# Chunk bounds as eight concurrent fp32 products over 576 queries, and a written-out order, in a chunk-selecting attention kernel with a phase mixer

## The chip, the cores and the metric

The kernel runs on one core of one Trainium2 chip. The metric is device time in microseconds from launch to end of one execution; a profile adds the span from the first to the last instruction, which is a little shorter. One core has five engines with a queue each: TensorE (PE; its weight loads are PEld), VectorE (DVE), ScalarE (ACT), GpSimd (POOL) and SyncE (SP, which issues the DMAs here).

## The reference: what is computed

For 4 batches and 8 heads, 768 positions and a head size of 64, each query chooses 6 of 24 chunks of 32 keys by an upper bound on its scores, and attends to the keys of the chosen chunks that are not after it:

```
k_min, k_max = min and max of k over each chunk of 32 keys
ub  = sum over d of max(q * k_min, q * k_max)          # [.., 768, 24]
ub  = where(chunk of query >= chunk, ub, -1e9)
sel = the 6 chunks with the largest ub
attn = softmax(where(sel and causal, q @ k.T / 8, -1e9)) @ v
```

The heads are then laid side by side to x of 4 x 768 x 512, and a mixer follows:

```
theta = x @ w_theta
y = w_tok_r @ (x * cos(theta)) + w_tok_i @ (x * sin(theta))
u = x + y
out = u + max(u @ w_ch, 0)
```

Everything comes in and goes out as fp32. The bounds decide which chunks are chosen, so they are computed in fp32; scores and mixer run in fp16 with fp32 accumulation.

## The kernel before

The work is cut into tasks: `Plan.add` records for each one its engine (or a choice of ACT and DVE), an estimated duration, a key, what it reads and writes, and the buffers it takes. `Plan.order` then plays the tasks through a list scheduler: at each step it takes, among the engines, the task that can start first, and among equals the one with the smaller key. The table `SHIFT` moves the keys of named groups of tasks and biases the choice between ACT and DVE. `Plan.emit` writes the instructions in the order found, and on the chip each engine takes its own instructions in that order.

PSUM has three rings of buffers: "sc" (two, for scores), "av" (one, for attention times values) and "mi" (three banks, for everything else). The stages are:

- `load_kc`, `load_q`, `load_v`: DMAs for a group of four heads (batch b, half g) or a pair of heads.
- `keys`: VectorE takes maximum and minimum over each chunk in a tree (L411, L416, L420); TensorE transposes them (psk, L435); they become `bnd`, with dimension on the partitions, two heads of a pair on the two partition halves (L440). GpSimd casts the keys, and TensorE transposes them (pkt) into `kext`.
- `queries`: TensorE transposes q of a head pair in fp32 (psq, L485). ACT or DVE splits it into two parts by sign with a Relu (`ubq`, L493 and L495), so that the bound becomes two matrix products: one part with the maxima, one with the minima.
- `choice`: for a group of four heads, TensorE multiplies `bnd` by `ubq` (psub, L517), ACT or DVE copies the result to `ubm` (L525), TensorE transposes it back (psut, L532), and VectorE adds the causal mask (L537), finds the eight largest (L547) and compares with the sixth (L558). The result goes beside the cast queries and is turned by a DMA transpose into `qext`, where it acts as a mask inside the score product.
- `attend`: for each of 32 heads, scores (psc, L622), exp on ACT (pt, L631), a triangle mask on GpSimd (L642), the product with the values (psav, L653), a division on VectorE into x (L664, L669).
- `phases`: x transposed (psT, L688), theta (pst, L708), cos and sin on ACT, multiplied by x on VectorE (zz, L722).
- `mixer`: the token products (psy or, in the last batch, psz: L749, L751), u = x + y on VectorE (L761), u transposed (psut, L772, or a DMA), the channel product (pso, L784), the last addition (ot, L789), and the store.
- `token`: a token weight is loaded, cast on GpSimd (a, L809) and transposed (pw, L816).

The mixer of batch b runs between the heads of batch b + 1; the mixer of the last batch stands alone at the end. There are eight groups (b, g) for `choice`. A query in the first 192 positions sees at most six chunks, so it chooses all it may see. The kernel before leaves out the first 128 queries for that reason and covers the other five blocks of 128 in two parts of 256 and 384 columns:

```python
PARTS = ((1, 2), (3, 4, 5))
...
for y in range(2):
    for z, u in enumerate(us):
        nc.tensor.matmul(t[64 * z:64 * z + 64, :],
                         bnd[g][:, y, 2 * z:2 * z + 2, :].rearrange("p x c -> p (x c)"),
                         st[u][:, y, c0:c0 + w], start=(y == 0), stop=(y == 1))
```

Each such matmul contracts over all 128 partitions, which hold both heads of a pair. The sign constant `signs` makes one half of the partitions carry a maximum where the other carries a minimum, and the other way round in the second y.

Of the kernel before, what the change touches and what calls it, by code (L numbers as in the profile page):

```python
# [9 lines left out]
FP32 = mybir.dt.float32  # L10
# [6 lines left out]
class Task:  # L17
    __slots__ = ("i", "eng", "dur", "fn", "key", "deps", "succ", "alloc", "uses", "opts", "lock", "psum",
                 "after_start", "left", "ready", "start", "end", "kind", "group", "bias")


class Plan:
# [9 lines left out]

    LAT = {"PE": 0.22, "ACT": 0.08, "DVE": 0.08, "POOL": 0.08, "SP": 2.0}

    def __init__(self, bufs, in_order, hot, boost, shift):
        self.tasks = []
        self.bufs = bufs
        self.in_order = in_order
        self.count = {}
        self.hot, self.boost = hot, boost  # L40
        self.shift, self.group = shift, None
        self.turn = {}
        self.writers, self.readers = {}, {}
        self.tag_of, self.users = {}, {}

    def add(self, eng, dur, key, fn, r=(), w=(), new=(), after=(), kind=None, lock=False):
        t = Task()
        t.i, t.eng, t.dur, t.fn, t.key, t.kind = len(self.tasks), eng, dur, fn, key, kind
        t.opts = eng if isinstance(eng, dict) else {eng: dur}
        t.lock = lock or eng == "POOL"  # L50
        t.key += self.shift.get(self.group, 0.0)
        t.group = self.group
        t.bias = self.shift.get(("dve", self.group), 0.0)
        t.deps, t.after_start, t.succ, t.alloc, t.uses = set(), set(), [], [], []
        for name, tag in new:
            self.tag_of[name] = tag
            self.turn[name] = self.count.get(tag, 0)
            self.count[tag] = self.turn[name] + 1
            self.users[name] = []
            t.alloc.append(name)  # L60
        names = [n for n, _ in new]
        t.psum = [n[0] for n in r if isinstance(n, tuple) and self.tag_of.get(n[0]) in self.hot]
        if isinstance(eng, dict) or eng in ("ACT", "DVE"):
            if t.psum:
                t.key -= self.boost
        else:
            t.psum = []
        for n in list(r) + list(w) + names:
            base = n[0] if isinstance(n, tuple) and n and n[0] in self.users else n
            if base in self.users and t not in self.users[base]:  # L70
                self.users[base].append(t)
                t.after_start.add(self.users[base][0].i)
                t.uses.append(base)
        for n in r:
            t.deps |= set(self.writers.get(n, ()))
            self.readers.setdefault(n, []).append(t.i)
        for n in list(w):
            t.deps |= set(self.readers.get(n, ()))
            t.deps |= set(self.writers.get(n, ()))
            self.writers[n] = [t.i]  # L80
            self.readers[n] = []
        for n in names:
            self.writers[n] = [t.i]
        t.deps |= set(a.i for a in after)
        t.deps.discard(t.i)
        t.after_start -= t.deps | {t.i}
        self.tasks.append(t)
        return t

    def order(self):  # L90
        T = self.tasks
        for t in T:
            t.left = len(t.deps) + len(t.after_start)
            t.ready = 0.0
            t.start = None
            for d in t.deps:
                T[d].succ.append(t.i)
            for d in t.after_start:
                T[d].succ.append(t.i)
        placed = {}  # L100
        pending = {}
        freed, last = {}, {}
        for n, us in self.users.items():
            pending[n] = len(us)
        free_at = dict.fromkeys(("PE", "ACT", "DVE", "POOL", "SP"), 0.0)
        mode = [None]
        cand = {e: [] for e in free_at}
        for t in T:
            if t.left == 0:
                for e in t.opts:  # L110
                    cand[e].append(t)
        reader, port = {}, 0.0
        n_done, seq = 0, []
        now = 0.0

        def begin(t, e):
            s = max(free_at[e], now, t.ready, port if t.lock else 0.0)
            for n in t.psum:
                if n in reader and reader[n][0] != e:
                    s = max(s, reader[n][1] + 0.1)  # L120
            return s

        while n_done < len(T):
            best = None
            for e, c in cand.items():
                at = max(free_at[e], now)
                pick = None
                for t in c:
                    s = begin(t, e)
                    ok = True  # L130
                    if len(t.opts) > 1:
                        mine = s + t.opts[e] + (t.bias if e == "DVE" else 0.0)
                        for o, d in t.opts.items():
                            if o != e and begin(t, o) + d + (t.bias if o == "DVE" else 0.0) < mine:
                                ok = False
                    own = {}
                    for n in t.alloc:
                        tag = self.tag_of[n]
                        ring = placed.setdefault(tag, [])
                        m = len(ring) + own.get(tag, 0)  # L140
                        own[tag] = own.get(tag, 0) + 1
                        if tag in self.in_order and self.turn[n] != m:
                            ok = False
                            break
                        k = m - self.bufs[tag]
                        if k >= 0:
                            f = freed.get(ring[k])
                            if f is None:
                                ok = False
                                break  # L150
                            s = max(s, f)
                    if not ok:
                        continue
                    if pick is None or (max(s, at + 1e-9), t.key, t.i) < pick[0]:
                        pick = ((max(s, at + 1e-9), t.key, t.i), s, t)
                if pick and (best is None or pick[1] < best[1]):
                    best = pick + (e,)
            assert best is not None, "no task can start"
            _, s, t, _ = best
            for e in t.opts:  # L160
                cand[e].remove(t)
            t.eng = best[3]
            d = t.opts[t.eng]
            if t.kind is not None:
                if mode[0] not in (None, t.kind):
                    d += 1.3
                mode[0] = t.kind
            t.start, t.end = s, s + d
            now = s
            free_at[t.eng] = t.end  # L170
            if t.lock:
                port = t.end
            for n in t.psum:
                reader[n] = (t.eng, max(t.end, reader.get(n, (0, 0.0))[1]))
            lat = self.LAT[t.eng]
            for n in t.alloc:
                placed[self.tag_of[n]].append(n)
            for n in t.uses:
                pending[n] -= 1
                last[n] = max(last.get(n, 0.0), t.end + lat)  # L180
                if pending[n] == 0:
                    freed[n] = last[n]
            for i in t.succ:
                u = T[i]
                u.left -= 1
                same = t.eng != "SP" and list(u.opts) == [t.eng]
                u.ready = max(u.ready, t.start if t.i in u.after_start else t.end + (0.0 if same else lat))
                if u.left == 0:
                    for e in u.opts:
                        cand[e].append(u)  # L190
            seq.append(t)
            n_done += 1
        return seq

    def emit(self):
        for t in self.order():
            t.fn(t.eng) if len(t.opts) > 1 else t.fn()
# [3 lines left out]
def kernel(  # L201
# [19 lines left out]
    NM = 5  # L221
    scale = float(1.0 / np.sqrt(D))
# [17 lines left out]
    qt = P + np.arange(NM)[None, :, None] * P + np.arange(P)[:, None, None]  # L240
    cm_np = np.where(qt // CH >= np.arange(NCH)[None, None, :], 0.0, -1e9).astype(np.float32)
    cm_h = nc.inline_tensor(cm_np.reshape(P, NM * NCH), name="cmask32")
# [5 lines left out]
    cmask32 = const.tile([P, NM, NCH], FP32, name="cmask32", tag="c_cm")  # L248
# [103 lines left out]
    def act_t(n):  # L352
        return 0.19 + n / 1200.0
# [602 lines left out]
```

The softmax here doesn't subtract the row's maximum and nothing guards it: scores larger than these inputs give would overflow.

## Time and profile before

| what | value |
|---|---|
| time, median of 3 runs | 272.23 us (272.11 to 273.69) |
| span of the profiled execution | 270.0 us |
| mean granted TensorE clock | 0.968 |
| psub matmuls L517 | 128 records, 20.8 us busy |
| psut transposes L532 | 40 records, 273 ns median |
| scores L622 | 256 records, 51.7 us busy |
| token products L749 and L751 | 240 records, 45.5 and 45.4 us busy |
| first and last start of psub | 15.8 and 190.3 us |

The page gives for each engine its busy time, its share of the span and its instructions, and then the span in 40 equal slices. Busy time is an average over stages with different limits, so the span has to be cut where the work changes before anything is read from it. Matmuls overlap in the pipeline: the sum of their durations is more than the busy time.

### The profile page before, as it was taken

Reading aid. Unit: us, or ns where it says so; the run is one execution under the profiler, and the core shown is the slowest. Engines: PE = TensorE matmul, PEld = TensorE weight load, DVE = VectorE, ACT = ScalarE, POOL = GpSimd, SP = SyncE. Lnnn points to the kernel's source line nnn. Section 1 sums busy time; section 2 is a strip of 40 time slices with the busy share of each in tenths; the row PEclk is TensorE's granted clock in tenths of the full one; section 3 lists DMA queues with packets and bytes.
Section 4 is the critical chain, followed back from the end, with each engine's and each line's share of the span. In section 5 each row is a group of like instructions: output and inputs, shape, how many; then the busy total and the mean of one; then the engine's idle time right before and its main releaser. Section 6 shows DMA issues by size and latency. Waiting matters only on the chain.

```text
span 270.0 us, 5519 instructions
## 1 busy us (share of the span) xinstructions
PE 240.8 (89%) x2055; PEld 147.8 (55%) x2055; DVE 195.5 (72%) x474; ACT 162.0 (60%) x225; POOL 135.0 (50%) x188
## 2 busy tenths in 40 slices
PE   4896586978689989989999999999999999899993
PEld 1553355666434676655763477666654667434441
DVE  3959689899799594799999985997853436344453
ACT  2349647489559499271938879635687777374000
POOL 7534657668368886968642278536302555100000
PEclk9999598999869999999999999999999999999999
DMA  7897857799989789898988642337180014310123
GB/s 198 199 240 156 213 123 113 199 259 243 252 220 258 191 232 210 185 242 211 257 204 203 121 98 62 70 89 177 22 197 0 19 41 94 141 58 0 41 78 117
DMA packets 90434, 40.71 MB, mean 151 GB/s; under 512 B 83736, under 2 KB 83864, under 8 KB 89736
## 3 DMA queue, kind: packets, MB, share of 16 engines
q1 hardware_dynamic: 90408, 40.37, 61.5%
q8 instruction: 16, 0.26, 0.4%
q14 instruction: 10, 0.08, 0.1%
HBM read 26.20 MB, written 6.29 MB: 120 GB/s over the span
## 4 chain that ended last, share of the span: by engine, by line
PE 56%; DMA 16%; DVE 13%; POOL 8%; issue 3%; SPq 2%; ACT 1%; POOLq 0%; DVEq 0%; ACTq 0%
PE psy L749 8%; PE psy L751 8%; PE psc L622 8%; PE pso L784 6%; PE psub L517 5%; PE psav L653 5%; DMA w<-in_moe_w_tok_r_dram 4%; POOL pt L642 4%; DMA out_dram<-ot 4%; PE pst L708 4%; DMA q<-in_q_dram 3%; DMA w<-in_moe_w_tok_i_dram 3%; PE psq L485 2%; POOL a L809 2%; DVE h L411 2%
## 5 line engine op out<-in xcount | busy, mean ns | idle before, releaser
L631 ACT ACTIVATE pt<-psc 128x1024 f16<-128x1024 f32 (+1 forms) x96 | 83.8, 920 | 37.5 <-PE psc L622 36.4
L642 POOL TENSOR_TENSOR pt<-pt,tri 128x256 f16<-128x256 f16 x96 | 68.3, 722 | 56.8 <-ACT pt L631 55.6
L622 PE MATMUL psc<-qext,kext 88*128 88x512 f16 (+3 forms) x256 | 51.7, 317 | 2.4 <-ACT pt L631 1.6
L749 PE MATMUL psy<-zz,wtokT 128*128 128x512 f16 x120 | 45.5, 379 | 0.9 <-DVE ot L789 0.9
L751 PE MATMUL psy<-zz,wtokT 128*128 128x512 f16 x120 | 45.4, 379 | 0.0
L622 PEld LDWEIGHTS <-kext 88*128 88x128 f16 x256 | 33.8, 153 | 13.6 <-issue 4.1
L653 PE MATMUL psav<-v,pt 128*128 128x65 f16 x672 | 28.0, 194 | 2.2 <-POOL mm L429 2.1
L653 PEld LDWEIGHTS <-pt 128*128 128x128 f16 x672 | 25.3, 98 | 7.9 <-POOL pt L642 2.9
L708 PE MATMUL pst<-wtheta,xT 128*128 128x512 f16 x96 | 25.8, 410 | 1.2 <-ACT xT L693 0.5
L761 DVE TENSOR_TENSOR u<-psy,x 128x512 f16<-128x512 f32 x20 | 13.6, 688 | 16.3 <-PE psy L751 16.3
L411 DVE TENSOR_TENSOR h<-kc 96x1024 f32<-96x1024 f32 (+1 forms) x16 | 21.2, 1327 | 5.3 <-DMA kc<-in_k_dram 5.2
L789 DVE SCALAR_TENSOR_TENSOR ot<-pso,u 128x512 f32<-128x512 f32 x24 | 16.4, 688 | 11.7 <-PE pso L784 8.8
L784 PE MATMUL pso<-wch,uT 128*128 128x512 f16 x96 | 23.5, 379 | 0.6 <-DMA uT<-u 0.6
L751 PEld LDWEIGHTS <-wtokT 128*128 128x128 f16 x144 | 14.1, 98 | 15.9 <-issue 2.3
L493 ACT ACTIVATE ubq<-psq,signs 128x256 f32<-128x256 f32 (+1 forms) x30 | 14.0, 531 | 13.6 <-PE psq L485 13.5
L749 PEld LDWEIGHTS <-wtokT 128*128 128x128 f16 x144 | 14.1, 98 | 14.1
L722 DVE TENSOR_TENSOR zz<-x,cs 128x1024 f16<-128x1024 f16 x24 | 17.7, 755 | 4.8 <-ACT cs L716 4.6
L716 ACT ACTIVATE cs<-pst,pi 128x512 f16<-128x512 f32 x24 | 16.6, 693 | 7.2 <-DVE zz L722 4.9
L517 PE MATMUL psub<-ubq,bnd 128*64 128x384 f32 (+1 forms) x128 | 20.8, 463 | 0.1
L447 POOL CAST ke<-kc 96x1024 f16<-96x1024 f32 x16 | 17.4, 1097 | 6.4 <-DMA kc<-in_k_dram 6.2
L485 PE MATMUL psq<-ident,q 128*128 128x128 f32 x80 | 14.7, 310 | 5.7 <-DMA q<-in_q_dram 3.0
L475 POOL CAST qe<-q 128x768 f16<-128x768 f32 x16 | 16.1, 1010 | 6.1 <-DMA q<-in_q_dram 3.2
(69 smaller groups left out, 364.0 us busy)
## 6 DMA issues: line engine op xcount, KB each, us to landing
q<-in_q_dram SPq DMA_DIRECT2D x32, 192.0 KB, 3.6
v<-in_v_dram SPq DMA_DIRECT2D x64, 96.0 KB, 3.1
out_dram<-ot SPq DMA_DIRECT2D x24, 256.0 KB, 2.3
kc<-in_k_dram SPq DMA_DIRECT2D x7, 768.0 KB, 6.2
w<-in_moe_w_tok_r_dram SPq DMA_DIRECT2D x6, 384.0 KB, 4.7
w<-in_moe_w_tok_i_dram SPq DMA_DIRECT2D x6, 384.0 KB, 4.3
w<-in_moe_w_theta_dram SPq DMA_DIRECT2D x4, 256.0 KB, 2.7
w<-in_moe_w_ch_dram SPq DMA_DIRECT2D x4, 256.0 KB, 3.7
```

Source lines behind the costliest of these rows:

```text
L411: nc.vector.tensor_tensor(out=st[hn].rearrange("p (z w) d -> p z (w d)", z=2)[:, s], in0=kv[:, s, 0], in1=kv[:, s, 1], op=op)
L485: nc.tensor.transpose(t[:, o * P:(o + 1) * P], st[q32][:, n, :, :].rearrange("p x d -> p (x d)"), ident32)
L517: nc.tensor.matmul(t[64 * z:64 * z + 64, :], bnd[g][:, y, 2 * z:2 * z + 2, :].rearrange("p x c -> p (x c)"), st[u][:, y, c0:c0 + w], start ...
L622: nc.tensor.matmul(t[:, a0:a1], kx[0:KX, hj:CH * 96:NCH], qx[0:KX, q0 + a0 - o:q0 + a1 - o], start=True, stop=True)
L631: nc.scalar.activation(out=t[:, BASE[s]:BASE[s] + wa + wb], in_=st[psc][:, 0:wa + wb], func=AF.Exp, bias=0.0, scale=scale)
L642: nc.gpsimd.tensor_tensor(out=d, in0=d, in1=tri16.unsqueeze(1).broadcast_to([P, 2, P]), op=ALU.mult)
L653: nc.tensor.matmul(t[:, a, :], st[pt][:, o:o + P], v16s[g][:, x, j, :], start=(j == 0), stop=(j == a))
L708: nc.tensor.matmul(p, st[xT][:, c, t * P:(t + 1) * P], wtheta16[:, c, :], start=(c == 0), stop=(c == 3))
L722: nc.vector.tensor_tensor(out=st[zz][:, t, :, :], in1=st[cs], op=ALU.mult, in0=st[xx][:, t, :].unsqueeze(1).broadcast_to([P, 2, dm]))
L749: nc.tensor.matmul(acc(), wtokT16[:, i, 0, t * P:(t + 1) * P], st[zz][:, i, 0, :], start=(i == 0), stop=False)
L751: nc.tensor.matmul(acc(), wtokT16[:, i, 1, t * P:(t + 1) * P], st[zz][:, i, 1, :], start=False, stop=(i == NT - 1))
L784: nc.tensor.matmul(p, st[uT][:, c, :], wch16[:, c, :], start=(c == 0), stop=(c == 3))
```

## The change

There are two parts. The first rewrites `choice`. The bound products become sixteen matmuls per group: two signs y, and for each of them eight that lie on different parts of the TensorE array. A matmul takes one head of a pair (x, one half of 64 partitions), one pair (z) and one run of 320 queries (th), and gives 32 rows of the result. The two heads of a pair go to two PSUM tiles, the four combinations of run and pair to four quarters of the partitions. The queries now start at position 192 (`Q0`), so 576 of them remain; the two runs start at column 0 and column 256 of these. One run is 320 columns wide, so 64 columns are covered twice. Of the six blocks that come back from the transposes, one holds only the queries covered twice and is not used by the maxima.

The second part takes the list scheduler away. `ORDER` is a written list of all 1442 tasks; the sign of an entry says whether a task that may run on ACT or DVE runs on DVE. The list came from an annealing search. It holds another order on every engine, DMA issues included, and other choices between ACT and DVE.

```diff
+    Q0 = 6 * CH
+    QN = S - Q0
+    QW = QN - 2 * P
...
+    ubm = per.tile([P, 2, 3 * P], FP32, name="ubm", tag="ubm")
...
-        "ubq": ([P, 2, NM * P], FP32, 4), "ubm": ([P, NM * P], FP32, 1), "ubs": ([P, NM, 4, NCH], FP32, 1), "top8": ([P, NM, 4, 8], FP32, 1),
+        "ubq": ([P, 2, QN], FP32, 4), "ubs": ([P, 2, 6, 2, NCH], FP32, 1), "top8": ([P, 2, 6, 2, 8], FP32, 1),
...
-    SHIFT = {
...
+    ORDER = (
...
-        for i, blocks in enumerate(PARTS):
...
-                for y in range(2):
                     for z, u in enumerate(us):
-                        nc.tensor.matmul(t[64 * z:64 * z + 64, :],
-                                         bnd[g][:, y, 2 * z:2 * z + 2, :].rearrange("p x c -> p (x c)"),
-                                         st[u][:, y, c0:c0 + w], start=(y == 0), stop=(y == 1))
+        def mm():
+            ts = [newp(n, "mi", [P, QW], FP32) for n in psub]
+            for y in range(2):
+                for th in range(2):
                     for z, u in enumerate(us):
+                        for x in range(2):
+                            r = slice(x * D, (x + 1) * D)
+                            c = 32 * (2 * th + z)
+                            nc.tensor.matmul(ts[x][c:c + 32, :], bnd[g][r, y, 2 * z + x, :],
+                                             st[u][r, y, th * 2 * P:th * 2 * P + QW], start=(y == 0), stop=(y == 1))
...
+        for x in range(2):
+            psut = ("psut", b, g, x)
+
+            def cp(e, x=x):
+                (nc.scalar.copy if e == "ACT" else nc.vector.tensor_copy)(out=ubm[:, x, 3 * P - QW:], in_=st[psub[x]])
...
+                for a in range(3):
+                    nc.tensor.transpose(t[:, a, :], ubm[:, x, a * P:(a + 1) * P], ident32)
...
+                for a in (0, 2, 3, 4, 5):
+                    for z in range(2):
+                        nc.vector.max(out=t8[:, x, a, z, :], in_=st[ubs][:, x, a, z, :])
...
+                for a0, o in ((0, full[:, :, 0:3]), (3, full[:, :, 3:5])):
+                    n = 3 if a0 == 0 else 2
+                    nc.vector.tensor_tensor(
+                        out=o, in0=st[ubs][:, x, a0:6:2].rearrange("p a z c -> p z a c"),
+                        in1=st[top8][:, x, a0:6:2, :, 5:6].rearrange("p a z c -> p z a c").broadcast_to([P, 2, n, NCH]),
+                        op=ALU.is_lt)
...
     def emit(self):
-        for t in self.order():
-            t.fn(t.eng) if len(t.opts) > 1 else t.fn()
+        done = set()
+        for o in self.order:
+            t = self.tasks[~o if o < 0 else o]
...
+            if len(t.opts) > 1:
+                t.fn("DVE" if o < 0 else "ACT")
+            else:
+                t.fn()
```

## The prediction

> **What bounds the kernel now.** I read the page first, then the busy times cut into three stages at places that the timeline gives (the first psy matmul, at 83.6 us, and the first psz matmul, at 241.2 us), then the chain of waits inside the first stage, then the psub matmuls alone. The page:
>
> ```profile
> span 270.0 us, 5519 instructions
> PE 240.8 (89%) x2055; PEld 147.8 (55%) x2055; DVE 195.5 (72%) x474; ACT 162.0 (60%) x225; POOL 135.0 (50%) x188
> PEclk9999598999869999999999999999999999999999
> ```
>
> The three stages (columns: stretch, length, busy us of each engine with instructions, granted clock, DMA share, GB/s):
>
> ```profile
> 0.00:83.60 83.60, 63.68 (x528) 40.20 (x529) 68.32 (x161) 51.34 (x74) 50.40 (x75) 0.90 0.86 204
> 83.60:241.20 157.60, 152.87 (x1401) 96.24 (x1400) 114.18 (x294) 106.14 (x144) 84.58 (x114) 1.00 0.58 138
> 241.20:270.00 28.80, 24.25 (x129) 11.40 (x127) 12.99 (x21) 4.48 (x8) 0.00 (x0) 1.00 0.17 64
> ```
>
> The reader is to see two kernels in one. Up to 83.6 us TensorE idles for 20 us and runs at a clock of 0.90, while VectorE is busy for 68 of 84 us and the DMA engines for 0.86. After that TensorE is busy for 97% at full clock: there its own work is the time. The chain of waits over the end of stage one says what the early idling is made of:
>
> ```profile
> 56.02 5.97 DMA w<-in_moe_w_tok_r_dram
> ...
> 67.67 7.37 DMA w<-in_moe_w_tok_i_dram
> 75.05 0.02 issue
> 75.07 0.04 POOLq L809
> 75.11 0.08 issue
> 75.19 0.84 POOL a L809
> ...
> 79.54 5.16 DMA w<-in_moe_w_tok_r_dram
> ```
>
> GpSimd stands in its queue behind a cast of a token weight (L809) that has not landed, and the masks that attention needs (L642) stand behind that cast. Three such landings make 18.5 us of the chain. Last, the operation that is changed:
>
> ```profile
> L517 PEld LDWEIGHTS psub<-ubq,bnd x128: 132/137/232, 15.8 to 190.0; 128*64 128x64 f32 x128
> L517 PE MATMUL psub<-ubq,bnd x128: 379/486/817, 15.8 to 190.3; 128*64 128x256 f32 x64, 128*64 128x384 f32 x64
> ```
>
> The program has 64 such matmuls and the trace 128 records, two for each. Half of 128 times 379 and half times 486 ns make over 55 us, but the stage view gives these instructions 20.8 us of busy time (8.3 in stage one, 12.5 in stage two): records overlap. Two head pairs already run side by side in two column halves of the array.
>
> **What the Trainium skill says.** "FP8 and Floating Point Precision", section "TensorE Precision Notes", states that true fp32 takes four passes through the array; two records of two passes each fit that. "TensorE: Matmul & The Clock Gate", section "Part 3: Packing small matmuls — row/col tiling", states that matmuls on different row and column tiles run at the same time, starting some 4 ns apart; the trace of before agrees for two column tiles (the overlap above), and no record of before shows row tiles. "TensorEngine Tiling (Array Packing)", section "Gotcha 1: PSUM Pressure", says that different row tiles must write to different PSUM banks; the new code does so, with one psub tile for each head parity, and so takes two of the three "mi" banks at once.
>
> **The change part by part.**
>
> 1. *The products.* In the chain of waits the four 256-column matmuls of one group take 1.01 us and the four 384-column ones 1.44 us, or 2.31 us together where they follow each other. The difference is 0.43 us for 128 columns, 3.36 ns per column for two rounds (y = 0, 1), with 0.15 us beside it. Now each round is eight tiles of 64 rows and 32 columns at once, over 320 columns instead of 640. If all eight share the array, a group takes 320 x 3.36 ns + 0.15 = 1.23 us. If only four run together it is twice the stream, 2.30 us; if only two, 4.45 us. I take 1.23, since two column tiles lose nothing today, and keep the others for the range. The contraction over 64 rows instead of 128 loses nothing by itself: a zero half is no longer multiplied.
>
> 2. *The transposes of the bounds*: six in place of five per group. The chain has 0.58 us for five, so +0.12. Parts 1 and 2 make 2.31 - 1.23 - 0.12 = 0.96 us less TensorE per group, 7.7 us for eight groups. The first two groups lie in the slow-clock stretch (the second takes 3.48 us), but stage one is not TensorE's.
>
> 3. *VectorE.* Per group: two casts of the bounds into ubs of 288 elements (0.446 us each) instead of 192 and 288 (0.352 + 0.446), +0.09; the selection compare (L558) in four pieces instead of two, from medians of 0.35 and 0.45 to perhaps 0.30 and 0.25 twice, +0.3; the 20 maxima and the two copies of psub keep their size; the Relu parts lose 64 of 640 columns, under 0.1 us per group on either engine. So +0.4 per group, 3 us in all. Against this the fixed order gives the Relu parts to ACT 45 times instead of 30 (VectorE 19 instead of 34) and 22 kext copies to ACT instead of 18: 15 x 0.54 + 4 x 0.55 = 10 us go from VectorE to ACT, as some 11 us there. In stage two VectorE is busy 72% and ACT 67%: neither ends it, and TensorE's own work hides both changes.
>
> 4. *The waits added.* All parts of a query pair must be there before the one product starts, where before the first 256 columns could go ahead; both banks are held until their copies end, so a third user of "mi" that stands behind psub on TensorE waits for one copy (0.48 us). In the new order score and value matmuls, which have banks of their own, stand behind psub in most groups and cover that. I cost it at 0.1 us per group at most, 0.8 with the wait for all parts.
>
> 5. *The order.* It replaces the planner's choice on every engine. I counted TensorE work along both program orders, with the start-to-start distances that the trace shows at full clock (0.216 us for 512 columns of psy, pso and pst, 0.032 for one psav, 0.22/0.109/0.056 for scores, 0.11 for a 128-column fp32 transpose). Before: 219.0 us in all, 48.0 ahead of the first psy, 147.1 from there to the first psz, 23.8 after. Now: 211.3 us; 48.2, 138.5 and 24.7. So stage one has the same TensorE work although it now holds four groups of chunk bounds instead of three, and stage two has 8.6 us less. VectorE has 58.4 us of work ahead of the first zz before and 60.4 now, +2. The transposes of token weights ahead of the first psy fall from 36 to 24, that is from six landed and cast weights to four: each of the landings quoted is 5 to 7 us of the chain, so two fewer could give 10, but v, q and k loads share the DMA engines, and most of it is then queued elsewhere. I take 4 off for that against the 2 of VectorE: stage one -2.
>
> The tail: 0.9 us more work is left for it, but the last eight pso matmuls now stand between the last psy and its transposes, covering the VectorE pass (0.69) that TensorE waits for today; with psT and pst interleaved with pso I make it -0.5 in all.
>
> Sum: -2 - 8.6 + 0 to 0.8 of part 4, which I put inside the 4.7 us that TensorE idles in stage two already, - 0.5 = -11.1. From 272.2 that is **261**.
>
> **The rivals.** *The order gives more.* If two fewer token landings shorten stage one by 8 rather than 2 us, and two of the 4.7 us of idle in stage two go, the time is 253. For it: stage one has 20 us of idle TensorE and a clock of 0.90. Against: VectorE has 60 us of work there, and DMA is at 0.86. *The array shares less than eight ways.* Four at a time leaves 2.30 us, so each group costs 0.1 more than before instead of 0.96 less; stage two's 8.6 us shrink by about 5 x 1.07 to 3.3, and the time is 267. Two at a time costs 4.45 - 1.23 = 3.2 us per group more than forecast, five groups in stage two: 261 + 16 = 277, slower. For it: each partition now feeds four fp32 streams at once instead of two, and no record shows that; against: two cost nothing. *The fixed order blocks.* Every engine takes its work in the written order. If ACT, with 11 us more, now holds up scores, and each psub pair blocks the third bank in stage two, TensorE idles there as it does in stage one (24% instead of 3%): a quarter of that change over 157 us is 8 us, and with a stage one longer by 6 from the loads put differently, the time is 261 + 14 = 275, slower. For it: the chain of stage one already shows one late operation blocking a whole queue; against: in stage two the order keeps independent score and value work behind every product.
>
> **How the numbers follow.** Forecast 261 (256 to 266): 0.50. More from the order, 253: 0.20. Four at a time, 267: 0.10. Slower, 275 to 277, by blocking or by two at a time: 0.15. About even, a small gain eaten: 0.05. Faster by over 1% (under 269.5): 0.50 + 0.20 + 0.10 = 0.80; within 1%: 0.05; slower: 0.15. For eight in ten the range leaves out the lowest tenth below 250 and the slower cases above 273.
>
> **What would show it.** Right: psub busy of about 10 us in all, with a group near 1.2 us; TensorE busy down by 6 to 10 us; the stretch from first psy to first psz near 149 us and still 97% busy at full clock; first psy at 80 to 84 us. A psub group of 2.3 us or more shows that the tiles do not share the array; a stage two with TensorE under 94% busy shows blocking, and the waits then name ACT pt or a psub copy; a first psy before 77 us shows that the order carried more than the products. A time above 272 proves the forecast wrong.

## The result, and the profile after

The changed kernel takes 260.13 us (median of 4 runs, 259.9 to 260.99) where the kernel before takes 272.96 us (4 runs, 272.11 to 275.13). The ratio is 0.952, with a 95% interval of 0.946 to 0.959. The forecast was 261.

The page of the kernel after, its head:

```profile
span 259.2 us, 5799 instructions
PE 232.8 (90%) x2191; PEld 144.7 (56%) x2191; DVE 184.2 (71%) x470; ACT 172.7 (67%) x246; POOL 131.8 (51%) x188
PEclk9999659779999999999999999999999999999999
```

The same three stages, cut at the first psy matmul (84.6 us) and the first psz matmul (229.1 us). Columns: stretch, length, then the busy us of PE, PEld, DVE, ACT and POOL with their instructions, the granted clock, the DMA share, GB/s:

```profile
0.00:84.60 84.60, 64.38 (x648) 41.86 (x648) 68.59 (x188) 58.16 (x89) 52.72 (x77) 0.90 0.99 207
84.60:229.10 144.50, 143.05 (x1413) 91.10 (x1412) 103.77 (x265) 106.60 (x146) 79.09 (x111) 1.00 0.69 148
229.10:259.20 30.10, 25.38 (x133) 11.77 (x131) 11.81 (x18) 7.98 (x14) 0.00 (x0) 1.00 0.16 61
```

Against the kernel before, stage one is 1.0 us longer (83.6), stage two 13.1 us shorter (157.6), the tail 1.3 us longer (28.8). The whole gain shows in the stage that TensorE bounds, where TensorE is now busy for 99% instead of 97%. Stage one looks untouched, but it is not: it now does the chunk bounds of four groups instead of three, which puts 188 instructions on VectorE into it instead of 161. On ACT there are 89 instead of 74, mostly because ACT now takes 26 of the Relu parts there instead of 14.

The changed product itself, by line:

```profile
L419 PEld LDWEIGHTS psub<-ubq,bnd x256: 102/107/174, 16.7 to 195.4; 64*32 64x32 f32 x128
L419 PE MATMUL psub<-ubq,bnd x256: 429/429/740, 16.7 to 195.6; 64*32 64x320 f32 x128
```

and one group of it in the timeline (columns: start, length, what, count):

```profile
167.49 1.31 PE L419 MATMUL psub<-ubq,bnd 64*32 64x320 f32 x32
```

The 32 records, most of 429 ns, fit into 1.31 us. The single records show how: eight start 7 ns apart (0, 7, 13, ... 47 ns), the next eight at 293 to 340 ns, then at 562 and 832 ns. Eight tiles share the array, and a group takes four rounds of 0.27 us. (The prediction quotes some 4 ns between starts; here they are 7 ns apart.) Seven of the eight groups take 1.31 us; the third takes 2.39 us, in a stretch in which the granted clock is 0.50. In the kernel before, a group took 2.37 us in the same view at full clock.

The chain of waits at the end of stage one, where landings of token weights stood before:

```profile
64.50 0.90 ACT pt L534 x2
65.40 8.13 DMA qext<-qe
73.57 1.04 PE psc L525 x6
```

The three landings of 5 to 7 us are off the chain; one turn of the queries by DMA, of 8.13 us, stands in their place.

### The profile page after: what moved, and what is told of

Read it like the earlier page. It is cut to its first block, busy times and chain, and to the rows that moved or that the text cites. A ratio compares the mean times of both kernels' runs of the same rounds, so it can differ in the third digit from the quotient of the medians.

```text
span 259.2 us, 5799 instructions
## 1 busy us (share of the span) xinstructions
PE 232.8 (90%) x2191; PEld 144.7 (56%) x2191; DVE 184.2 (71%) x470; ACT 172.7 (67%) x246; POOL 131.8 (51%) x188
## 2 busy tenths in 40 slices
DMA packets 90436, 40.74 MB, mean 157 GB/s; under 512 B 83609, under 2 KB 83865, under 8 KB 89737
## 4 chain that ended last, share of the span: by engine, by line
PE 72%; DVE 15%; DMA 7%; issue 3%; ACT 2%; SPq 1%; ACTq 0%; DVEq 0%
PE psc L525 13%; PE psy L652 10%; PE psy L654 10%; PE psav L556 7%; PE pst L611 7%; PE pso L687 7%; PE psub L419 4%; DMA qext<-qe 3%; PE psq L386 3%; DVE h L311 3%; DMA q<-in_q_dram 3%; DVE top L448 2%; PE psz L652 2%; PE psz L654 2%; PE psut L433 2%
## 5 line engine op out<-in xcount | busy, mean ns | idle before, releaser
L534 ACT ACTIVATE pt<-psc 128x1024 f16<-128x1024 f32 (+1 forms) x96 | 84.9, 919 | 29.7 <-PE psc L525 27.8
L525 PE MATMUL psc<-qext,kext 88*128 88x512 f16 (+3 forms) x256 | 54.6, 326 | 6.6 <-DVE qext L489 2.3
L556 PEld LDWEIGHTS <-pt 128*128 128x128 f16 x672 | 29.3, 100 | 9.6 <-POOL a L712 1.9
L556 PE MATMUL psav<-v,pt 128*128 128x65 f16 x672 | 31.8, 196 | 1.4 <-DVE x L572 1.3
L394 ACT ACTIVATE ubq<-psq,signs 128x384 f32<-128x384 f32 (+1 forms) x45 | 21.2, 507 | 17.5 <-PE psq L386 16.7
L625 DVE TENSOR_TENSOR zz<-x,cs 128x1024 f16<-128x1024 f16 x24 | 17.1, 718 | 11.1 <-ACT cs L619 10.9
L611 PE MATMUL pst<-wtheta,xT 128*128 128x512 f16 x96 | 24.2, 378 | 0.1
L311 DVE TENSOR_TENSOR h<-kc 96x1024 f32<-96x1024 f32 (+1 forms) x16 | 20.0, 1252 | 4.9 <-DMA kc<-in_k_dram 4.7
L386 PE MATMUL psq<-ident,q 128*128 128x128 f32 x80 | 15.3, 302 | 6.5 <-DMA q<-in_q_dram 4.2
L375 POOL CAST qe<-q 128x768 f16<-128x768 f32 x16 | 14.3, 894 | 12.6 <-DMA q<-in_q_dram 6.6
L361 ACT COPY kext<-pkt 64x768 f16<-64x768 f16 x22 | 17.4, 793 | 3.2 <-PE pkt L355 2.8
```

The lines of the kernel that those rows point to most:

```text
L311: nc.vector.tensor_tensor(out=st[hn].rearrange("p (z w) d -> p z (w d)", z=2)[:, s], in0=kv[:, s, 0], in1=kv[:, s, 1], op=op)
L386: nc.tensor.transpose(t[:, o * P:(o + 1) * P], st[q32][:, n, :, :].rearrange("p x d -> p (x d)"), ident32)
L394: nc.scalar.activation(out=o, in_=i_, func=AF.Relu, bias=0.0, scale=signs[:, y:y + 1])
L525: nc.tensor.matmul(t[:, a0:a1], kx[0:KX, hj:CH * 96:NCH], qx[0:KX, q0 + a0 - o:q0 + a1 - o], start=True, stop=True)
L534: nc.scalar.activation(out=t[:, BASE[s]:BASE[s] + wa + wb], in_=st[psc][:, 0:wa + wb], func=AF.Exp, bias=0.0, scale=scale)
L556: nc.tensor.matmul(t[:, a, :], st[pt][:, o:o + P], v16s[g][:, x, j, :], start=(j == 0), stop=(j == a))
```

## The experiments

All ratios are to the kernel before on the same chip; that of the changed kernel is 0.952. The medians of the kernel before beside these runs lie between 273.1 and 274.3 us, so small differences between times in this section are to be read from the ratios. Stages are cut in each kernel as above, at its first psy and its first psz matmul.

**The products without the order.** The new `choice` under the list scheduler of before, with its table of shifts.

```diff
-    ORDER = (
-    ...
-    )
-    PHK = -2
+    SHIFT = {
+    ...
+    }
+    BOOST, PHK = 0, -2
```

> The new products under the list scheduler and its old table of shifts, without the written order. If both parts of the change count (the theory), the products alone give the 0.96 us per group in the four to five groups that lie in the TensorE-bound stretch and up to 2 us before it: 266 to 268 us, with TensorE busy down by about 8 us. If the written order does it all: 271 to 274, as before. If the products do it all: 260 to 262. The table was tuned for other tasks, so a time above 272 would say that the scheduler's choice is spoilt by small changes of duration, and not that the products cost time; psub busy near 11.5 us then still shows them cheap.

It takes 283.86 us, ratio 1.034 (1.028 to 1.040). TensorE is busy for 239.9 us in it, next to the 240.8 of before, at a lower mean clock (0.946 instead of 0.968). Its stages:

```profile
0.00:90.90 90.90, 67.07 (x674) 43.71 (x675) 73.71 (x197) 57.30 (x86) 59.53 (x82) 0.91 0.97 214
90.90:253.20 162.30, 148.57 (x1390) 92.45 (x1390) 109.24 (x267) 103.20 (x140) 77.63 (x107) 0.96 0.53 120
253.20:282.00 28.80, 24.31 (x129) 11.43 (x127) 13.04 (x22) 4.47 (x8) 0.00 (x0) 1.00 0.17 64
```

Six of its eight product groups take 1.31 us and the two others 2.0 and 2.4 us at a granted clock of 0.65 and 0.50, so the products are as cheap as in the changed kernel. The time is lost elsewhere: TensorE idles 13.7 us in stage two, where the changed kernel has 1.5, and stage one is 6.3 us longer, with DMA landings of 3.6 (queries), 3.6 (theta weights) and 9.2 us (a token weight) on its chain. The waits of TensorE in stage two are spread, none above 2.6 us in all, so no single cause is shown; that the table of shifts was made for the old tasks is the likely one. The run doesn't price the products; the next one does.

**The order without the products.** The old two-column products in the written order, task for task, with the same engines (the two parts of a product stand together, and the copy `ubm` is one fixed tile, as in the changed kernel).

```diff
-    SHIFT = {
-    ...
-    }
+    ORDER = (
+    ...
+    )
...
     def emit(self):
-        for t in self.order():
...
+        for o in self.order:
+            t = self.tasks[~o if o < 0 else o]
...
```

> The old products (two column tiles, two parts, 640 queries) in the written order, task for task, with the same choice of ACT and DVE. Theory: the stretch from the first psy to the first psz holds four groups and gets 4 x 0.96 us longer, the stretch before it at most 2 us: 264 to 266 us. If the products do it all: 270 to 272. If the order does it all: 260 to 261.

It takes 270.38 us, ratio 0.9875 (0.984 to 0.991), 4 to 6 us slower than my theory said and in the range of the rival by which the products do it all, though the interval leaves the order a share. Its stages:

```profile
0.00:88.60 88.60, 67.54 (x579) 44.36 (x580) 69.35 (x180) 58.94 (x89) 52.58 (x77) 0.87 0.86 198
88.60:237.90 149.30, 146.66 (x1345) 93.02 (x1344) 102.47 (x256) 107.14 (x146) 78.30 (x111) 1.00 0.63 143
237.90:268.00 30.10, 25.38 (x133) 11.72 (x131) 11.81 (x18) 7.97 (x14) 0.00 (x0) 1.00 0.16 61
```

This run splits the result. From the kernel before to this one, the order alone: stage one +5.0, stage two -8.3, tail +1.3. From this one to the changed kernel, the products within the order: stage one -4.0, stage two -4.8, tail 0. So within this order the products are worth 1.0 to 1.2 us a group in *both* stages, and the 1.0 us by which stage one grew is +5.0 of the order, which brings work forward, and -4.0 of products. It is one way to split the gain: with the products first, as in the run above, there is no gain to split.

The chains of waits over stage one show why the products count there. They are the psub pieces of the kernel before, of this run, and of the changed kernel, the last with the piece in which VectorE makes the bounds for its third product:

```profile
15.85 2.31 PE psub L517 x16
32.52 3.48 PE psub L517 x16
```

```profile
16.57 2.30 PE psub L447 x16
39.77 2.31 PE psub L447 x16
53.39 3.69 PE psub L447 x16
68.70 2.31 PE psub L447 x16
```

```profile
16.75 1.24 PE psub L419 x32
38.93 1.24 PE psub L419 x32
...
49.91 0.36 DVE bnd L340
...
50.42 2.39 PE psub L419 x32
```

All four old products of this stage stand in the chain, 10.6 us together. In the changed kernel three do, with 4.9 us, and the chain passes by the fourth, through the turn of the queries.

**The product twice.** In the changed kernel, each product of the first two batches, or of the last two, is computed twice in place.

```diff
+            for _ in range(2 if b < 2 else 1):
                 for y in range(2):
                     for th in range(2):
...
```

For the last two batches the condition is `b > 1`.

> The changed kernel with each product of the four groups of the first two batches computed twice in place (the second pass overwrites the first), 4 x 1.1 us more TensorE work, all of it before the first psy matmul. Theory: that stretch is set by VectorE and DMA, so 0 to 2 us more, 260 to 262. Rival (TensorE time counts the same everywhere): 264.5 to 265.

> The same for the four groups of the last two batches, all of which lie between the first psy and the first psz matmul. Theory: TensorE is the time there, so all of 4 x 1.1 us shows: 264 to 265. Rival (the 6 us of idle TensorE in that stretch take it up): 260 to 262.

Early: 264.75 us, ratio 0.968 (0.962 to 0.973); late: 265.48 us, ratio 0.968 (0.963 to 0.973). The stage that holds the doubled products, of the early and of the late kernel:

```profile
0.00:88.60 88.60, 69.02 (x775) 44.95 (x776) 70.13 (x188) 58.55 (x89) 52.25 (x77) 0.87 0.97 199
```

```profile
85.30:234.60 149.30, 146.92 (x1542) 93.72 (x1541) 102.34 (x265) 106.90 (x146) 77.85 (x111) 1.00 0.62 143
```

Stage one grows by 4.0 us in the first, stage two by 4.8 us in the second, and stages two and three of the early kernel keep their length (144.5 and 30.1). For the late one my theory holds. For the early one its rival does: 1.1 us more per group comes out as 1.0 us although TensorE idles 20 us in that stage. The product is a link between two pieces of VectorE work there, the bounds before it and the copies and maxima after it, and all four doubled products stand in this kernel's chain (2.31, 2.31, 4.04 and 2.31 us). Its length is waited for even where its engine idles.

**Does it matter which tiles stand next to each other?** The sixteen matmuls of a group in two other orders: both signs of four tiles before the other four, and both signs of one tile before the next tile.

```diff
-            for y in range(2):
-                for th in range(2):
+            for th in range(2):
+                for y in range(2):
                     for z, u in enumerate(us):
                         for x in range(2):
```

```diff
-            for y in range(2):
-                for th in range(2):
-                    for z, u in enumerate(us):
-                        for x in range(2):
+            for th in range(2):
+                for z, u in enumerate(us):
+                    for x in range(2):
+                        for y in range(2):
```

> The changed kernel with the product's loops turned round: both signs of the first run of queries, then both of the second, so that only four different tiles (two row halves by two column quarters) stand next to each other. If matmuls keep their order and a tile has to finish its two signs first, eight rounds of 0.27 us instead of four: psub near 2.4 us a group. As the doubled products showed that 1.1 us a group counts everywhere, the time is then that of the two doublings together, 260 + 4 + 4.5 = 268 to 269. Rival (each tile has a queue of its own, so order in the program does not matter): 1.3 us a group and 260 to 261.

> The changed kernel with the two signs innermost: each tile's two matmuls follow each other, so that neighbours in the program always share a tile. If matmuls start strictly in the program's order, a tile's later passes hold up the next tile and a group takes between 3 and 6 us; each us a group costs 8 us in all, so 274 us or more. Rival (tiles run ahead on their own): 1.3 us a group and 260 to 261.

Both expectations fell, and the rival holds, with 1.33 and 1.35 us a group and times slightly above its 260 to 261: 261.66 us, ratio 0.961 (0.957 to 0.965), and 262.86 us, ratio 0.965 (0.960 to 0.969). One group of the tile-by-tile kernel in the timeline:

```profile
167.27 1.35 PE L419 MATMUL psub<-ubq,bnd 64*32 64x320 f32 x32
```

Its records start at 0, 13, 27, 39, 53, 66, 79 and 93 ns, and the next eight only from 293 ns on. In the program the second sign of a tile comes before the first of the next tile; on the chip the eight first passes still come 13 ns apart, twice the 7 ns of the changed kernel, and the rest later. The starts fit tiles that run ahead of each other while a later pass waits for its own tile, and this order costs 0.04 us a group. The profiled executions have spans of 259.8 and 259.1 us, next to 259.2 in the changed kernel; the medians are 1.5 and 2.7 us higher, with runs from 260.9 to 266.2 us for the second, and what makes those runs longer is not shown.

**Is stage one bound by the amount that DMA moves?** Token weights load 64 of their 768 columns, and the cast repeats them. The mixer then works with other weights, so the kernel computes something else at the same work for every engine.

```diff
-        dma(..., lambda: nc.sync.dma_start(out=new(n), in_=wtok[t * P:(t + 1) * P, :]), nw=[n])
+        dma(..., lambda: nc.sync.dma_start(out=new(n)[:, 0:D], in_=wtok[t * P:(t + 1) * P, 0:D]), nw=[n])
...
-        plan.add(..., lambda: nc.gpsimd.tensor_copy(out=new(a), in_=st[n]), ...
+        plan.add(..., lambda: nc.gpsimd.tensor_copy(
+            out=new(a).rearrange("p (c d) -> p c d", d=D), in_=st[n][:, 0:D].unsqueeze(1).broadcast_to([P, 12, D])), ...
```

> The changed kernel with token weights that load 64 of 768 columns and repeat them in the cast (the mixer then uses other weights, the work of every engine stays). 4.3 MB of 40 are not moved, some 2 MB of them before the first psy matmul. If the DMA engines bound that stretch, as their share of 0.99 says, it gets 6 to 10 us shorter: 251 to 255 us. If they only look full (VectorE, the chain through TensorE and the turns bound it): under 2 us, 258 to 261.

It takes 262.06 us, ratio 0.959 (0.952 to 0.966), no faster than the changed kernel. Its first stage:

```profile
0.00:85.00 85.00, 63.92 (x648) 41.93 (x649) 68.93 (x187) 58.31 (x89) 51.60 (x78) 0.90 0.97 186
```

It moves 21 GB/s less and is as long (85.0 and 84.6 us). The 8.13 us turn of the queries is off the chain, which passes through the fourth product instead, and TensorE's wait for turns falls from 1.8 to 0.4 us, yet the stage keeps its length: the chain that takes its place is about as long. So stage one is not set by the amount that is moved. Whether it is set by the DMA engines in another way stays open, since the number of packets is the same (90,435 and 90,436 in all) and the busy share hardly falls, from 0.99 to 0.97. That share is no measure of the amount either: the old products in the written order move the same 17.5 MB in stage one (198 GB/s over 88.6 us, next to 207 over 84.6) at a share of 0.86.

**The choice between ACT and VectorE.** In the written order, entries change sign, and nothing else (a negative entry -n stands for task n - 1 on VectorE, so `-65` is task 64): 11 of the 22 Relu parts that ACT has in the first two batches go to VectorE; or 12 of 23 in the last two; or, the other way, the seven that VectorE has in the first two batches after the first group go to ACT.

```diff
-        ... 30, 31, 18, 64, 67, 72, 15, 69, 70, 73, 61, 63, 71, ...
+        ... 30, 31, 18, -65, 67, 72, 15, 69, 70, 73, 61, -64, 71, ...
```

These are two of the 11 entries of the first run.

> The changed kernel with every second of the Relu parts that ACT has in the first two batches (11 of 22) given back to VectorE, at the same place in the order: 6 us of work move from ACT to VectorE before the first psy matmul. If VectorE bounds that stretch (81% busy), 3 to 6 us more: 263 to 266. If not, within 1 us of the changed kernel.

> The changed kernel with every second of the Relu parts that ACT has in the last two batches (12 of 23) given back to VectorE, at the same place in the order, where TensorE is busy 99%. The prediction costs the choice between ACT and VectorE at nothing there: within 1 us of the changed kernel, 259 to 262. Rival (as in the first two batches, where 11 parts cost 11 us: a later eviction holds up TensorE's banks): 265 or more.

> The other direction: the seven Relu parts of the first two batches that VectorE still has after the first group go to ACT, 3.7 us of work off VectorE before the first psy matmul. If VectorE's amount of work bounds that stretch, 2 to 4 us less: 256 to 258. If the place of each part in the order counts, and not the amount, the same or longer: 260 to 265.

Early to VectorE: 271.12 us, ratio 0.992 (0.988 to 0.996), some 11 us for 6 us of work. Late to VectorE: 266.66 us, ratio 0.974 (0.969 to 0.979), 6 us for 6. Early to ACT: 261.26 us, ratio 0.955 (0.948 to 0.962), no gain. In the first of them the waits of TensorE in stage one name the parts that were moved (columns: us in total, times, longest):

```profile
PE psq L387 <- DVE ubq L397: 3.3, 3, 2.1
PE psk L336 <- DVE ubq L397: 2.7, 1, 2.7
...
PE pkt L356 <- DVE ubq L397: 1.9, 1, 1.9
...
PE psT L592 <- DVE ubq L397: 1.7, 1, 1.7
```

A Relu part empties a bank of "mi". At the same place in the order but on VectorE it comes later, and TensorE's next transposes wait for it: 9.6 us in all, where the changed kernel waits 3.9 us in stage one for Relu parts on either engine (the profiled execution took 275.6 us, 4.5 above the median). In the late kernel it is the division that comes late, in a stage where the changed kernel shows no such wait:

```profile
PE psav L557 <- DVE x L573: 2.9, 2, 2.0
```

That stage is 6.3 us longer (150.8): TensorE idles 5.2 us in it instead of 1.5, and is busy for 2.5 us more at a granted clock of 0.99 instead of 1.00. The moved parts are not hidden by TensorE's own work, as step 3 of the prediction had it.

**More VectorE work, nothing moved.** The selection compares of the first two batches done twice.

```diff
-                for a0, o in ((0, full[:, :, 0:3]), (3, full[:, :, 3:5])):
+                for a0, o in ((0, full[:, :, 0:3]), (3, full[:, :, 3:5])) * (2 if b < 2 else 1):
```

> The changed kernel with the selection compares of the first two batches done twice, four groups of some 0.76 to 1.5 us: 4 us more VectorE work before the first psy matmul, nothing moved from another engine. If VectorE bounds that stretch: 3 to 4 us more, 263 to 265. If it has room (16 us idle there): under 1 us, 260 to 261.

It takes 266.16 us, ratio 0.973 (0.966 to 0.979), between 5 and 6 us for the 4.0 added. Stage one is 3.0 us longer (87.6), and stage two, in which 2 of the 16 added compares fall, 3.5 us:

```profile
0.00:87.60 87.60, 66.38 (x648) 43.41 (x649) 71.79 (x201) 58.64 (x88) 55.54 (x77) 0.84 0.99 201
87.60:235.60 148.00, 143.13 (x1413) 91.07 (x1412) 107.66 (x268) 106.95 (x146) 79.28 (x111) 1.00 0.66 144
```

TensorE's work in stage two is the same 143.1 us; what is added is idling, 4.9 us instead of 1.5. Most of it is one wait, which ends 6.8 us into the stage:

```profile
PE psy L652 <- DVE zz L625: 2.8, 1, 2.8
```

The first token products have used up the phases that are ready, and wait for the next ones from a VectorE that is late. So work added on VectorE in stage one counts in full, and part of it only shows behind the stage's end. Seven Relu parts taken off VectorE gained nothing, but they went to ACT, so no run shows what less work in all would give.

**The order with the old engines.** For every task with a choice, the engine that the list scheduler took in the kernel before; 77 of 1443 tasks (one more than was said ahead of the prediction) change sides, 49 to VectorE and 28 to ACT. The edit is again the sign of entries.

> The changed kernel with the list scheduler's choice between ACT and VectorE for every task that may run on either (77 tasks change sides, 44 to 49 of them to VectorE), in the written order of places. If order and choice of engine belong together, as the two runs that gave Relu parts back to VectorE suggest, this is slower than the kernel before: 275 to 285. If the choice is free (the prediction's step 3), 260 to 262; if only the amount of VectorE work counts (some 9 us more), 265 to 270.

It takes 288.62 us, ratio 1.051 (1.041 to 1.060), some 27 us more than the changed kernel by the two ratios, and beyond what I expected of the worst case. Its stages one and two:

```profile
0.00:97.00 97.00, 72.32 (x646) 45.36 (x647) 70.69 (x194) 54.48 (x79) 53.60 (x79) 0.77 0.89 188
97.00:258.00 161.00, 148.29 (x1414) 92.59 (x1413) 110.39 (x277) 101.30 (x135) 78.01 (x110) 0.98 0.60 128
```

VectorE has 194 us of work in all and ACT 162, no more than in the kernel before. Next to the changed kernel VectorE has 10 us more, for 27 us of loss, so the amount alone doesn't explain it; the rest is lost with the fit of places and engines. Of the 12.4 us by which stage one is longer, TensorE idles for 4.5, and for 7.9 it is busy, at a granted clock of 0.77 instead of 0.90. What lowers the clock is not shown.

## Why the prediction was right, and where it was not

The time (261 forecast, 260.1 measured) and the sum came out: -11.1 forecast, -10.8 between the two spans. The price of the products was right; that the whole sum came out so closely was luck: stage one came 3.0 us worse than forecast, the tail 1.8 us worse, and stage two 4.5 us better.

1. *The products*: right. 1.23 us a group forecast from the chain of waits, 1.24 measured in it at full clock. The saving of 0.96 us a group measured 1.2 in stage two and 1.0 in stage one (order without products against the changed kernel).
2. *"Stage one is not TensorE's", so the products count little there*: wrong. They are worth 4.0 us there, shown by the old products in the new order and again by the early doubling. I had read TensorE's idle time as room. The chain of before has two products in that stage, of 2.31 and 3.48 us, and that was the place to look. The first psy matmul came at 84.6 us, just outside the 80 to 84 that were to show the forecast right.
3. *Two token landings fewer take 4 us off stage one*: not borne out. The landings are off the chain in the written order, with the new products and with the old, but with the old the stage is 5.0 us longer, and with token loads of a twelfth of the size it is as long as in the changed kernel. Stage one was forecast at -2 and measured +1.0, made of +5.0 for work brought forward and -4.0 for the products. What fills those 5.0 us is not split further: a fourth group of bounds lies in the stage, and the run without the products has 15 more ACT and 19 more VectorE instructions in it than the kernel before, with ACT busy for 7.6 us more.
4. *Stage two, -8.6*: mis-sized. It measured -13.1. By my count TensorE's work there fell by 8.6 us as forecast, and its idle beside that count fell from 10.5 to 6.0 us, which I had left unchanged: 3.5 of these 4.5 us come with the order already (149.3 us for 142.3 of counted work, the 138.5 of the changed kernel and 4 x 0.96), the rest with the products.
5. *The choice between ACT and VectorE at nothing*: wrong as a rule. In this order 12 parts on the other engine cost 6 us in the TensorE-bound stage. It did no harm to the forecast because the order came with the choice that fits it.
6. *The tail, -0.5*: measured +1.3. The 0.9 us of work moved into it showed; the cover that the last pso matmuls were to give did not.

The rival "the order gives more" was right that idle time in stage two would go (3.5 us with the order) and wrong about stage one, which the order made longer. In the order in which these runs take the parts, the order alone gives 3.4 us (1.25% of 273), and the other three quarters are the products within it. "Four at a time" and "two at a time" fall with the starts 7 ns apart; their times in the prediction count five groups in stage two, where its own count of work leaves four. "The fixed order blocks" did not happen in the changed kernel, but the moved Relu parts, the doubled compares and the old engines show that a fixed order blocks as soon as durations or engines differ from those it was made for.

## What to carry to other kernels

Before you price a shorter operation at nothing because its engine idles in that stage, look whether it stands in the chain of waits: an operation between two pieces of another engine's work is waited for at full length. Small fp32 products shared the array eight ways at no loss here, and the gain showed in full both where their result is waited for and where TensorE is the bound. A written-out order and its choice of engines are one thing: change neither, nor a duration in it, without making the other anew, and don't judge an operation by putting it into an order that was tuned for its predecessor (the new products under the old table make a saving look like a loss of 3%).

## What the runs showed of the hardware that I had not expected

- Eight fp32 tiles (two row halves, four column quarters), each with its own stream, take no longer a round than the column rate of two tiles leads to: 0.27 us for 320 columns, 0.84 ns a column.
- Matmuls of different tiles need not wait for each other in the program's order: with both signs of a tile next to each other in the program, a group takes 1.35 instead of 1.31 us.
- A DMA busy share of 0.97 to 0.99 did not mean that the amount moved bounds the stage: 21 GB/s less left the length as it was and the share nearly so, and the same amount in the written order with the old products has a share of 0.86.
- The share of idle time in a stage does not tell the granted clock: TensorE idles 24% of stage one in the changed kernel, at 0.90, 25% with the old engines, at 0.77, and 26% with the products under the list scheduler, at 0.91. The low clock costs: with the old engines TensorE is busy 72 us there for work that takes 64 in the changed kernel.
